# Group normalization on one core: VectorE's and TensorE's unrolled code put into loops with addresses from registers

## The chip, the cores and the metric

The kernel runs on one core of one Trainium2 chip. The metric is the device time of one execution in microseconds (us). Five engines of the core work from their own instruction streams and meet through semaphores: TensorE (PE; its weight loads are listed as PEld), VectorE (DVE), ScalarE (ACT), GpSimd (POOL) and SyncE (SP), which here only issues transfers. Sixteen DMA engines move data between the chip's memory (HBM) and the on-chip memory (SBUF); PSUM is the memory into which TensorE writes.

## The reference

Input x has the shape 128 x 1024 x 32 x 16 in bf16 (134 MB); the output has the same. The 1024 channels form 32 groups of 32. For each image and group, mean and variance are taken over 32 x 32 x 16 = 16384 values; then every channel is scaled and shifted.

```python
xr = x.reshape(B, G, C // G, H, W)
mu = xr.mean(axis=(2, 3, 4), keepdims=True)
var = ((xr - mu) ** 2).mean(axis=(2, 3, 4), keepdims=True)
xn = (xr - mu) / jnp.sqrt(var + 1e-5)
xn = xn.reshape(B, C, H, W)
return xn * g[None, :, None, None] + b[None, :, None, None]
```

## The kernel before

A tile is four images: 128 partitions (image and group), and in each the 16384 values of one group, that is 32 channels of 512 values (KC = 32, HW = 512). One tile has 4 MB. There are NT = 32 tiles and NBUF = 6 buffers `xt0` to `xt5`, in which a tile is loaded, scaled in place and stored. Tile i lies in buffer (i + ENTRY) mod 6 with ENTRY = 4.

The work on one tile, in order:

- SP issues the load (L163), which raises the buffer's semaphore `ld`.
- TensorE adds up the tile: 32 matmuls of 512 columns with the identity matrix `eye` as weights accumulate into the PSUM tile `pa` of this buffer (L194). The last one raises `s_pe`.
- VectorE sums the 512 columns of `pa` and multiplies by -1/16384, which gives `negmean` (the function `mean`, L211), and raises `s_mean`.
- ScalarE takes the square of x - mean over the tile in two halves with accumulation (L316), and makes the standard deviation of it (L330, L337); it raises `s_std`.
- VectorE takes the reciprocal (L223), makes 32 factors `scl` (L226) and 32 offsets `bia` (L233), and scales the tile channel by channel with 32 tensor_scalar instructions of 128 x 512 (L243). The last one raises `s_dve`.
- SP issues the store (L171), which raises the buffer's semaphore `st`.

VectorE's order within a step is: the mean of the next tile first, then reciprocal, factors, offsets and scalings of this tile. So ScalarE has the next mean before VectorE starts on its scalings.

SP's queue is one list, written out by the function `sync_program`. It begins with six loads. Later it goes in groups: three stores, each of which waits for `s_dve`, then three loads, each of which waits until the store of the tile that had its buffer is complete; then a tiny transfer (`spare`, L157) with a wait for the one before. The last six tiles are stored one after the other with no loads between.

TensorE, VectorE and ScalarE each run a loop of six trips, made by the function `loop`. A trip is two blocks of unrolled code, `first` (buffers 0 to 3) and `second` (buffers 4 and 5); the first trip enters at `second`. At the end of a trip the semaphores are counted down (L134), a register is raised (L135) and a branch goes back (L136). On TensorE and VectorE (`ahead=True`) the set-up (`prepare`) stands behind the loop and is reached by branches. All addresses in the unrolled code are constants: every buffer has its own instructions, and VectorE has `rstd`, `scl` and `bia` once per buffer.

Of the kernel before, what the change touches and what calls it, by code (L numbers as in the profile page):

```python
# [8 lines left out]
ALU = mybir.AluOpType  # L9
ENG = mybir.EngineType  # L10
F32 = mybir.dt.float32
BF16 = mybir.dt.bfloat16
# [3 lines left out]
EPS = 1e-5  # L16

NBUF = 6
RUN = 3
MM_FREE = 512  # L20
ENTRY = 4
SPARE = 32

# [2 lines left out]
def kernel(  # L26
# [7 lines left out]
    nc = tc.nc  # L34
    P = nc.NUM_PARTITIONS
    B0, C, H, W = x.shape
    G = NUM_GROUPS
    HW = H * W
    assert P % G == 0 and C % G == 0
    NS = P // G  # L40
    assert B0 % NS == 0
    NT = B0 // NS
    KC = C // G
    F = KC * HW
    inv_n = 1.0 / float(F)
    NMM = F // MM_FREE
    TRIPS = (NT + ENTRY) // NBUF
    assert F % MM_FREE == 0 and NT + ENTRY == TRIPS * NBUF

    x_v = x.rearrange("(t n) (g k) h w -> t (n g) (k h w)", n=NS, g=G)  # L50
    o_v = out.rearrange("(t n) (g k) h w -> t (n g) (k h w)", n=NS, g=G)
# [3 lines left out]
    sb = ctx.enter_context(tc.tile_pool(name="sb", bufs=1))  # L55
    ps = ctx.enter_context(tc.tile_pool(name="ps", bufs=1, space=bass.MemoryType.PSUM))

    xt = [sb.tile([P, F], BF16, name=f"xt{j}") for j in range(NBUF)]
    ja = sb.tile([P, F // 2], FP8, name="ja")
    jd = [sb.tile([P, MM_FREE], BF16, name=f"jd{n}") for n in range(2)]  # L60
    gb_b = sb.tile([G, 2, KC], BF16, name="gb_b")
# [8 lines left out]
    sq = sb.tile([P, 2 * NBUF], F32, name="sq")  # L70
    half = sb.tile([P, NBUF], F32, name="half")
    std = sb.tile([P, NBUF], F32, name="std")
    rstd = sb.tile([P, NBUF], F32, name="rstd")
    scl = [sb.tile([P, KC], F32, name=f"scl{j}") for j in range(NBUF)]
    bia = [sb.tile([P, KC], F32, name=f"bia{j}") for j in range(NBUF)]
    pa = [ps.tile([P, MM_FREE], F32, name=f"pa{j}") for j in range(NBUF)]
    gb_p = ps.tile([P, 2, KC], F32, name="gb_p")

    def sem(name):
        return tc.alloc_semaphore(name)  # L80
# [4 lines left out]
    s_pe, s_mean, s_sq, s_std = sem("s_pe"), sem("s_mean"), sem("s_sq"), sem("s_std")  # L85
    s_spare = sem("s_spare")
    s_dd, s_dve = sem("s_dd"), sem("s_dve")

    def buf(i):
        return (i + ENTRY) % NBUF  # L90

    def col(t, j):
        return t[:, j % NBUF : j % NBUF + 1]

    def loop(engine, prepare, step, settle, counts, ahead=False):

        es = bass.OrderedEngineSet([engine.engine])
        name = f"trip_{engine.engine.name}"
        first, middle, over, second, leave, past, begin, end = (
            f"{name}_{part}"
            for part in "first middle over second leave past begin end".split()
        )
        trip = nc.alloc_registers(f"{name}_n", engines=es)

        def set_up():
            prepare()  # L110
            for s, _, n in counts:
                if n:
                    engine.sem_inc(s, n)
            nc.regs_mov(trip, 0)
            nc.br(second, engines=es)

        if ahead:
            nc.regs_mov(trip, -1)
            nc.br_lt(trip, -1, on_true=first, on_false=middle, engines=es)
        else:  # L120
            set_up()
        with nc.body(first, valid_engines=es):
            for j in range(ENTRY):
                step(j)
            nc.br(middle if ahead else second, engines=es)
        if ahead:
            with nc.body(middle, valid_engines=es):
                nc.br_lt(trip, 0, on_true=over, on_false=second, engines=es)
        with nc.body(second, valid_engines=es):
            for j in range(ENTRY, NBUF):  # L130
                step(j)
            settle()
            for s, n, _ in counts:
                engine.sem_inc(s, -n)  # L134
            nc.regs_alu(trip, trip, 1, op=ALU.add)  # L135
            nc.br_lt(trip, TRIPS, on_true=first, on_false=leave, engines=es)  # L136
        with nc.body(leave, valid_engines=es):
            nc.br(past if ahead else end, engines=es)
        if ahead:
            with nc.body(over, valid_engines=es):  # L140
                nc.br(past, engines=es)
            with nc.body(past, valid_engines=es):
                nc.br_lt(trip, TRIPS, on_true=begin, on_false=end, engines=es)
            with nc.body(begin, valid_engines=es):
                set_up()
        nc.switch_bb(end)

    spacers = [0]
# [28 lines left out]
    def tensor_program(pe):  # L177
        def prepare():
            pe.wait_ge(s_gb, 32)
            pe.wait_ge(s_rep, 1)  # L180
            pe.matmul(  # L181
                out=gb_p[:].rearrange("p a k -> p (a k)"),
                lhsT=rep[:],
                rhs=gb_b[:].rearrange("q a k -> q (a k)"),
                start=True,
                stop=True,
            ).then_inc(s_pe, 1)
            pe.wait_ge(s_eye, 1)

        def step(j):  # L190
            pe.wait_ge(ld[j], 16)
            pe.sem_inc(ld[j], -16)  # L192
            for k in range(NMM):
                m = pe.matmul(  # L194
                    out=pa[j][:],
                    lhsT=eye[:],
                    rhs=xt[j][:, k * MM_FREE : (k + 1) * MM_FREE],
                    start=(k == 0),
                    stop=(k == NMM - 1),
                )  # L200
            m.then_inc(s_pe, 1)

        loop(pe, prepare, step, lambda: None, [], ahead=True)
        pe.drain()
        pe.sem_inc(s_pe, 1)

    def vector_program(dve):
        gam, bet = gb[:, 0, :], gb[:, 1, :]

        def mean(j):  # L210
            dve.tensor_scalar(  # L211
                out=jd[j % 2][:],
                in0=pa[j % NBUF][:],
                scalar1=-inv_n,
                scalar2=None,
                op0=ALU.mult,
                op1=ALU.add,
                accum_out=col(negmean, j),
            )._wait_ge(s_pe, j + 2).then_inc(s_mean, 1)

        def step(j):
            mean(j + 1)
            dve.reciprocal(out=col(rstd, j), in_=col(std, j))._wait_ge(  # L223
                s_std, j + 1
            ).then_inc(s_dd, 1)
            dve.tensor_scalar(  # L226
                out=scl[j][:],
                in0=gam,
                scalar1=col(rstd, j),
                scalar2=None,  # L230
                op0=ALU.mult,
            )._wait_ge(s_dd, 3 * j + 2).then_inc(s_dd, 1)
            dve.scalar_tensor_tensor(  # L233
                out=bia[j][:],
                in0=scl[j][:],
                scalar=col(negmean, j),
                in1=bet,
                op0=ALU.mult,
                op1=ALU.add,
            )._wait_ge(s_dd, 3 * j + 3).then_inc(s_dd, 1)  # L240
            for k in range(KC):
                span = xt[j][:, k * HW : (k + 1) * HW]
                m = dve.tensor_scalar(  # L243
                    out=span,
                    in0=span,
                    scalar1=scl[j][:, k : k + 1],
                    scalar2=bia[j][:, k : k + 1],
                    op0=ALU.mult,
                    op1=ALU.add,
                )  # L250
                if k == 0:
                    m._wait_ge(s_dd, 3 * j + 4)
                if k == KC - 2 and j == NBUF - 1:
                    m.then_inc(s_dd, 1)
            m.then_inc(s_dve, 1)

        def settle():
            dve.wait_ge(s_dd, 3 * NBUF + 2)

        def prepare():  # L260
            dve.memset(ones_b[:], 1.0).then_inc(s_set, 1)  # L261
            dve.tensor_copy(out=gb[:], in_=gb_p[:])._wait_ge(s_pe, 1).then_inc(s_dd, 1)  # L262
            dve.sem_inc(s_pe, ENTRY)
            mean(ENTRY)

        loop(
            dve,
            prepare,
            step,
            settle,  # L270
            [
                (s_pe, NBUF, 0),
                (s_std, NBUF, ENTRY),
                (s_dd, 3 * NBUF + 1, 3 * ENTRY),
            ],
            ahead=True,
        )

    def pool_program(pool):
        pool.affine_select(  # L280
            out=eye[:],
            in_=ones_b[:],
            pattern=[[-1, P]],
            compare_op=ALU.is_equal,
            fill=0.0,
            base=0,
            channel_multiplier=1,
        )._wait_ge(s_set, 1).then_inc(s_eye, 1)
        pool.affine_select(  # L289
            out=rep[:].rearrange("q (n a) -> q n a", n=NS),  # L290
            in_=ones_b[0:G, :].rearrange("q (n a) -> q n a", n=NS),
            pattern=[[0, NS], [-1, G]],
            compare_op=ALU.is_equal,
            fill=0.0,
            base=0,
            channel_multiplier=1,
        ).then_inc(s_rep, 1)
        pool.tensor_scalar(  # L298
            out=eps_t[:],
            in0=ones_b[:, 0:1],  # L300
            scalar1=EPS,
            scalar2=None,
            op0=ALU.mult,
        ).then_inc(s_set, 1)

    def scalar_program(act):
        act.dma_start(out=gb_b[:, 0, :], in_=g_v).then_inc(s_gb, 16)
# [86 lines left out]
```

## Time and profile before

| what | value |
|---|---|
| time of the runs, median of 3 | 633.19 us (632.77 to 633.47) |
| profiled execution, its time | 633.13 us |
| its span, first to last instruction | 631.3 us |
| busy: TensorE / VectorE / ScalarE | 255.1 / 375.8 / 476.2 us |
| moved by DMA | 268.57 MB, mean 425 GB/s |
| mean granted clock of TensorE | 0.729 of full speed |

In the lines of the profile that the prediction shows, L243 is line 243 of the program before. A line of a group of instructions gives the line, the engine, the operation, output and input with partitions x elements, how many there were (x1024), then busy time in all and nanoseconds of one, and at the end the idle time of the engine just before them and what ended it. A line of a timeline or a chain begins with the start and the duration in us. In the row of DMA shares each digit is a fortieth of the span in tenths. A `q` behind an engine's name stands for its sequencer, which handles branches, register operations and the issue of transfers.

### The profile page before, as it was taken

The numbers are of one execution on the slowest core, as the hardware profiler recorded it, in microseconds if no ns is written. First come the engines' busy times: TensorE is split into PE (matmuls) and PEld (weight loads), VectorE is DVE, ScalarE is ACT, GpSimd is POOL, SyncE is SP. The second block draws the span as 40 slices with busy tenths as digits, with TensorE's granted clock in tenths as the row PEclk, the third lists the DMA queues.
The fourth block names the chain that finished last, engine by engine and source line by source line (L and its number), as shares of the span: only waits on it lengthen the run. The fifth ranks groups of instructions, "written<-read, shape, count | busy, mean of one in ns | idle before, by whom it ended". The sixth has DMA issues, their size and how long they took to land. (4 is left out here: it accounts for less than half of the span.)

```text
span 631.3 us, 3704 instructions
## 1 busy us (share of the span) xinstructions
PE 255.1 (40%) x1009; PEld 105.4 (17%) x1025; DVE 375.8 (60%) x1188; ACT 476.2 (75%) x194; POOL 0.9 (0%) x7
## 2 busy tenths in 40 slices
PE   0967409009602750582087018404720770095000
PEld 0423103003201320230032003101300230032000
DVE  0057777774772777077727735770777177447771
ACT  0499999995994699189929965993899199649930
POOL 0000000000000000000000000000000000000000
PEclk9998858658855985687578659855975796598555
DMA  8999999999999999999999999999999999999996
GB/s 363 432 432 414 434 432 432 438 432 432 430 432 434 430 430 434 432 430 432 432 432 432 432 432 430 432 432 432 430 432 434 432 430 432 432 432 436 438 394 283
DMA packets 10756, 268.57 MB, mean 425 GB/s; under 512 B 2560, under 2 KB 2560, under 8 KB 2560
## 3 DMA queue, kind: packets, MB, share of 16 engines
q1 hardware_dynamic: 10656, 268.52, 99.0%
q10 hardware_dynamic: 96, 0.00, 0.0%
q14 instruction: 3, 0.02, 0.0%
q8 instruction: 1, 0.02, 0.0%
HBM read 134.30 MB, written 134.22 MB: 425 GB/s over the span
## 5 line engine op out<-in xcount | busy, mean ns | idle before, releaser
L316 ACT ACTIVATE ja<-xt,negmean 128x8192 fp8e5<-128x8192 bf16 x64 | 455.5, 7117 | 126.9 <-DVE jd L211 125.5
L194 PE MATMUL pa<-xt,eye 128*128 128x512 bf16 x1008 | 254.9, 414 | 312.4 <-PEq L192 310.9
L243 DVE TENSOR_SCALAR xt<-xt,scl,bia 128x512 bf16<-128x512 bf16 x1024 | 333.7, 408 | 1.2
L194 PEld LDWEIGHTS pa<-xt,eye 128*128 128x128 bf16 x1024 | 105.3, 105 | 461.6 <-issue 366.0
L211 DVE TENSOR_SCALAR_CACHE_REDUCE jd<-pa 128x512 bf16<-128x512 f32 x33 | 22.7, 687 | 147.3 <-PE pa L194 145.4
L223 DVE RECIPROCAL rstd<-std 128x1 f32<-128x1 f32 x32 | 5.2, 163 | 78.1 <-ACT std L337 78.1
L316 ACT ACTIVATION_READ_ACCUMULATOR ja<-xt,negmean 128x1 f32 x64 | 11.9, 186 | 0.0
L337 ACT ACTIVATE std<-sq,half 128x1 f32<-128x1 f32 x32 | 9.4, 295 | 1.0
L330 ACT ACTIVATE half<-sq,eps_t 128x1 f32<-128x1 f32 x32 | 8.9, 278 | 0.0
L233 DVE SCALAR_TENSOR_TENSOR bia<-scl,negmean,gb 128x32 f32<-128x32 f32 x32 | 8.1, 252 | 1.1
L226 DVE TENSOR_SCALAR scl<-gb,rstd 128x32 f32<-128x32 f32 x32 | 7.7, 241 | 1.1
L262 DVE COPY gb<-gb_p 128x64 f32<-128x64 f32 x1 | 0.2, 226 | 10.7 <-PE gb_p L181 10.7
L181 PE MATMUL gb_p<-gb_b,rep 32*128 32x64 bf16 x1 | 0.2, 231 | 12.5 <-DMA gb_b<-in_b_dram 12.5
L211 DVE DVE_READ_ACCUMULATOR jd<-pa 128x1 f32 x33 | 2.7, 83 | 0.0
L312 ACT ACT_TABLE_LOAD x1 | 1.3, 1283 | 1.9 <-issue 1.9
L181 PEld LDWEIGHTS gb_p<-gb_b,rep 32*128 32x128 bf16 x1 | 0.1, 100 | 12.5 <-DMA gb_b<-in_b_dram 12.5
L261 DVE MEMSET ones_b<- 128x128 bf16 x1 | 0.2, 165 | 1.9 <-issue 1.9
L289 POOL TENSOR_SCALAR_AFFINE_SELECT rep<-ones_b 32x128 bf16<-32x128 bf16 x1 | 0.3, 303 | 0.0
L280 POOL TENSOR_SCALAR_AFFINE_SELECT eye<-ones_b 128x128 bf16<-128x128 bf16 x1 | 0.3, 294 | 1.7 <-DVE ones_b L261 1.7
L312 ACT ACTIVATE warm<-eps_t 128x1 f32<-128x1 f32 x1 | 0.2, 203 | 0.0
L298 POOL TENSOR_SCALAR eps_t<-ones_b 128x1 f32<-128x1 bf16 x1 | 0.2, 205 | 0.0
L378 POOL MEMSET const-uint8-127<- 128x1 uint8 x1 | 0.1, 103 | 0.0
(3 smaller groups left out, 0.3 us busy)
## 6 DMA issues: line engine op xcount, KB each, us to landing
xt<-in_x_dram SPq DMA_DIRECT2D x32, 4096.0 KB, 29.1
out_dram<-xt SPq DMA_DIRECT2D x32, 4096.0 KB, 33.2
spare<-in_x_dram SPq DMA_DIRECT2D x10, 8.0 KB, 29.2
gb_b<-in_g_dram ACTq DMA_DIRECT2D x1, 2.0 KB, 7.8
gb_b<-in_b_dram ACTq DMA_DIRECT2D x1, 2.0 KB, 11.0
```

Of the source, the lines that this page charges most:

```text
L181: pe.matmul(out=gb_p[:].rearrange("p a k -> p (a k)"), lhsT=rep[:], rhs=gb_b[:].rearrange("q a k -> q (a k)"), start=True, stop=True,).the ...
L194: m = pe.matmul(out=pa[j][:], lhsT=eye[:], rhs=xt[j][:, k * MM_FREE : (k + 1) * MM_FREE], start=(k == 0), stop=(k == NMM - 1),)
L211: dve.tensor_scalar(out=jd[j % 2][:], in0=pa[j % NBUF][:], scalar1=-inv_n, scalar2=None, op0=ALU.mult, op1=ALU.add, accum_out=col(negmean, j),
L223: dve.reciprocal(out=col(rstd, j), in_=col(std, j))._wait_ge(s_std, j + 1).then_inc(s_dd, 1)
L226: dve.tensor_scalar(out=scl[j][:], in0=gam, scalar1=col(rstd, j), scalar2=None, op0=ALU.mult,)._wait_ge(s_dd, 3 * j + 2).then_inc(s_dd, 1)
L233: dve.scalar_tensor_tensor(out=bia[j][:], in0=scl[j][:], scalar=col(negmean, j), in1=bet, op0=ALU.mult, op1=ALU.add,)._wait_ge(s_dd, 3 * j ...
L243: m = dve.tensor_scalar(out=span, in0=span, scalar1=scl[j][:, k : k + 1], scalar2=bia[j][:, k : k + 1], op0=ALU.mult, op1=ALU.add,)
L280: pool.affine_select(out=eye[:], in_=ones_b[:], pattern=[[-1, P]], compare_op=ALU.is_equal, fill=0.0, base=0, channel_multiplier=1,)._wait ...
L312: act.activation(out=warm[:], in_=eps_t[:], func=ACT.Sqrt)
L316: m = act.activation(out=ja[:], in_=xt[j][:, h * F // 2 : (h + 1) * F // 2], func=ACT.Square, bias=col(negmean, j), scale=1.0, accum_out=s ...
L330: act.activation(out=col(half, j), in_=sq[:, 2 * j : 2 * j + 1], func=ACT.Identity, bias=eps_t[:], scale=inv_n,)._wait_ge(s_sq, 3 * j + 1) ...
L337: act.activation(out=col(std, j), in_=sq[:, 2 * j + 1 : 2 * j + 2], func=ACT.Sqrt, bias=col(half, j), scale=inv_n,)._wait_ge(s_sq, 3 * j + ...
```

## The change

TensorE and VectorE get short loops whose addresses come from registers.

- The six buffers become parts of one tile `x_all`, and the six PSUM tiles parts of `pa_all`, so that a register can choose among them. `rstd`, `scl` and `bia` exist once.
- VectorE loses the loop of trips. It has one loop over the tiles (`i` from 4 to 35, buffer `j = i % NBUF` in a register) with one step in it, and in the step a loop of four rounds with eight channels each (`SCALE_STEP`). A drain follows the rounds, and it raises `s_dve`. The semaphores are counted down by one or by three inside the step.
- TensorE keeps the loop of trips with its blocks. In each tile the first and the last matmul stand alone with constant addresses; the 30 between are ten rounds of three (`MM_STEP`) with an address from a register.
- `ahead` and the blocks that it needed are gone from `loop`; the set-up stands ahead of the loop. The gamma and beta matmul raises a semaphore of its own, `s_gbp`.
- POOL, ScalarE and SP have the same instructions in the same order.

In the program that is built, addresses are worked out by packed register instructions, each of which holds several additions and multiplications. In a round of VectorE each of the eight tensor_scalar instructions has two of them ahead (six and two operations; seven and three for the first of a round), and takes four addresses from registers; then follow one register addition and a compare-and-branch. In a round of TensorE there are three packed ones (six, five and five operations), a separate register addition for the first matmul, and a register addition and a compare-and-branch at the end. In VectorE's step there are further a packed one of six with a modulo and one of two ahead of the mean, a packed one of three ahead of the reciprocal, a register addition ahead of the offsets, and a register move and branch ahead of the rounds.

The core of the diff:

```diff
-    xt = [sb.tile([P, F], BF16, name=f"xt{j}") for j in range(NBUF)]
+    x_all = sb.tile([P, NBUF * F], BF16, name="x_all")
+    xt = [x_all[:, j * F : (j + 1) * F] for j in range(NBUF)]
...
+    rstd = sb.tile([P, 1], F32, name="rstd")
+    scl = sb.tile([P, KC], F32, name="scl")
+    bia = sb.tile([P, KC], F32, name="bia")
...
     def step(j):
         pe.wait_ge(ld[j], 16)
         pe.sem_inc(ld[j], -16)
-            for k in range(NMM):
-                m = pe.matmul(
...
+            add(xt[j][:, 0:MM_FREE], start=True)
+            with nc.Fori(0, (NMM - 2) // MM_STEP, 1, engines=...) as r:
+                for n in range(MM_STEP):
+                    add(xt[j][:, bass.ds((r * MM_STEP + n + 1) * MM_FREE, MM_FREE)])
+            add(xt[j][:, F - MM_FREE : F], stop=True).then_inc(s_pe, 1)
...
+        mean(ENTRY, 1)
+        with nc.Fori(ENTRY, NT + ENTRY, 1, engines=es) as i:
+            j = i % NBUF
+            mean((i + 1) % NBUF)
+            dve.reciprocal(out=rstd[:], in_=at(std, j, 1))._wait_ge(s_std, 1).then_inc(
+                s_dd, 1
+            )
+            dve.sem_inc(s_std, -1)
...
+            dve.wait_ge(s_dd, 3)
+            dve.sem_inc(s_dd, -3)
+            with nc.Fori(0, KC // SCALE_STEP, 1, engines=es) as r:
+                for n in range(SCALE_STEP):
+                    k = r * SCALE_STEP + n
+                    span = at(x_all, j * KC + k, HW)
+                    dve.tensor_scalar(
+                        out=span,
+                        in0=span,
+                        scalar1=at(scl, k, 1),
+                        scalar2=at(bia, k, 1),
+                        op0=ALU.mult,
+                        op1=ALU.add,
+                    )
+            dve.drain()
+            dve.sem_inc(s_dve, 1)
```

## The prediction

> **What bounds the kernel now.** I read the profile's page first, then the timeline of the DMA queue, the chain that ended last and a table by stage of the last 20 us. From the page:
>
> ```profile
> span 631.3 us, 3704 instructions
> PE 255.1 (40%) x1009; PEld 105.4 (17%) x1025; DVE 375.8 (60%) x1188; ACT 476.2 (75%) x194; POOL 0.9 (0%) x7
> ...
> DMA  8999999999999999999999999999999999999996
> ...
> L243 DVE TENSOR_SCALAR xt<-xt,scl,bia 128x512 bf16<-128x512 bf16 x1024 | 333.7, 408 | 1.2
> ...
> L223 DVE RECIPROCAL rstd<-std 128x1 f32<-128x1 f32 x32 | 5.2, 163 | 78.1 <-ACT std L337 78.1
> ```
>
> The DMA engines are full from the second slice to the last but one; no compute engine is over 75%. The timeline of SP's queue has the rhythm:
>
> ```profile
> 405.61 19.68 SPq L163 DMA_DIRECT2D xt<-in_x_dram  x3
> 425.34 0.43 SPq L157 DMA_DIRECT2D spare<-in_x_dram  x1
> 425.81 30.42 SPq L171 DMA_DIRECT2D out_dram<-xt  x3
> 464.00 19.68 SPq L163 DMA_DIRECT2D xt<-in_x_dram  x3
> ```
>
> Six transfers of one tile pass in 464.00 - 405.61 = 58.4 us, 9.73 us each, so a tile (in and out) costs the DMA 19.47 us. Transfers run in order: the first of the loads issued from 405.61 lands at about 434.7 (TensorE starts it then), the third at 454, two stores follow, and the third store, issued at 456.2, has its place only at about 474. Compute is some 17.5 us ahead of the DMA in mid-kernel, and VectorE is free to take up to 19.47 us a tile there. It takes 11.8 (mean 0.70, reciprocal to first scaling 0.76, scalings 10.43), and waits 3.07 for ScalarE, whose pace is 14.87 us a tile.
>
> At the ends there is no such cover. The chain that ended last:
>
> ```profile
> 553.47 7.12 PE pa L194 x28
> ...
> 560.61 0.71 DVE jd L211 x2
> ...
> 606.85 10.43 DVE xt L243 x32
> ```
>
> and the table by stage (columns: window; us; busy time of PE, PEld, DVE, ACT, POOL; clock; DMA share; GB/s):
>
> ```profile
> 614.00:616.00 2.00, 0.00 (x0) 0.00 (x0) 2.00 (x8) 0.00 (x0) 0.00 (x0) 0.50 0.27 115
> 616.00:618.00 2.00, 0.00 (x0) 0.00 (x0) 1.28 (x4) 0.00 (x0) 0.00 (x0) 0.50 0.27 115
> 618.00:620.00 2.00, 0.00 (x0) 0.00 (x0) 0.00 (x0) 0.00 (x0) 0.00 (x0) 0.50 1.12 475
> ```
>
> The DMA runs dry from 614 to 618: the last store waits for the last scaling (617.3). So what is added between the landing of tile 29 (551.8) and 617.3 is added to the span.
>
> The price of a sequencer's register instruction comes from the loop edges:
>
> ```profile
> L135 PEldq ALU_OP  x6: 36/36/42, 27.8 to 575.9; - x6
> ...
> L135 DVEq ALU_OP  x6: 40/40/58, 66.1 to 617.3; - x6
> ```
>
> Start to start in the trace's records, an ALU_OP of VectorE takes 78 ns (162.871 to 162.949), of PE 102 (106.608 to 106.710); a semaphore increment of VectorE 95. A taken branch on VectorE: 305 ns from its start (162.949) to the next operation's (163.254); a branch not taken, 81 (617.359 to 617.440). PE's taken branch executes 208 ns, about 250 to the next start.
>
> **The change, part by part.** It moves no DMA and no ScalarE instruction; SP, POOL and ScalarE keep their order.
>
> *VectorE's scaling.* The 32 tensor_scalar instructions stay, at 323 ns start to start (41.408 to 41.731), but each now has in front of it two packed register instructions (six and two operations, giving four addresses). No trace here shows such a packed one. Bounds: the six cost between one ALU_OP (78) and six (468); I take 78 + 5 x 13 = 143, a third of the 40 ns execution for each further operation, as fetch is paid once. The two: 78 to 156, taken 91. Issuing the tensor_scalar itself: 78 (an ALU_OP) to 323 (the sequencer keeps up now); with four addresses from registers I take 160. Sum 0.39 us, taken 0.40; bounds 0.234 (the engine's 0.323 then decides) and 0.947. I stay nearer the low end, because the nearest row is one whole instruction, and 38 of its 78 ns are not execution and here paid once for several operations. Each of four rounds ends with an ALU_OP, a taken branch (305, less the issue already counted) and two more packed operations: about 0.33, so 1.3 a tile (0 if queued work covers it, 1.5 at most). The loop: 32 x 0.40 + 1.3 = 14.1, +3.7 on 10.43.
>
> [...]
>
> *Around it, once a tile.* Before the first scaling: two semaphore decrements (0.095 each), a wait for the third s_dd, a register move, a branch, a packed pair, an issue; partly beside the small operations: 0.8 (0.3 to 1.5). They queue ahead of the scalings, for which the store waits. At the tile's end: drain, ALU_OP, taken branch, two packed instructions with the modulo, issue of the mean: 0.8 (0.4 to 1.5), before 0. So VectorE needs D = 0.70 + 1.55 + 14.1 + 0.8 = 17.15 us a tile: over ScalarE's 14.87, under the DMA's 19.47.
>
> *TensorE.* A round of three matmuls has three packed instructions, two ALU_OPs, a taken branch. With 145 for a packed one (36 execution + 66 fetch + 4 x 11) and 100 for the matmul with its weight load: 3 x 245 + 204 + 250 = 1.19 us; ten rounds and the rest 12.4 us a tile. Now the first tile of a burst takes 9.24 (15.00 to 24.24), starting at half clock (428 ns a matmul, later 216). So +3.0; low 0 (the sequencer keeps ahead), high 2.73 us a round with all 16 packed operations at 102, 27 us a tile. In mid-kernel +3.0 lies under the 17.5; only tiles 0 and 29 count.
>
> *The rest at nothing:* one rstd, scl and bia instead of six, since VectorE runs in order; the set-up without its detour (branches of 0.1 us, under the first load's 15 us).
>
> *Sum.* Start: store 0 was ready at 51.2, now 51.2 + 3.0 + 0.8 + 3.7 = 58.7, before its place at 62.3 (six loads). Store 1 follows one D later, 75.85; issue and first bytes take 1.8; the DMA is free at 72.0: 5.6 idle. Store 4 at 75.85 + 3 x 17.15 + 1.8 = 129.1, its place (120.6 + 5.6) is 126.2: 2.9 idle. Together 8.5. After that VectorE, faster than the DMA, falls behind no further. End: the mean of tile 29 is 3.0 later; from there to the last scaling it took 617.28 - 560.61 = 56.7, now four VectorE steps less the last turn, 4 x 17.15 - 0.8 = 67.8: +11.1. Span 631.3 + 8.5 + 3.0 + 11.1 = 653.9. The profiled execution took 633.13, 1.8 over its span (median of the runs 633.19), so **656 us**. With s from 0.34 to 0.47 us a scaling this case runs from 640 to 680.
>
> **Rivals.**
> *VectorE's sequencer keeps ahead* (s at most 0.33). For: the 0.234 bound, and queued scalings that would hide the round ends. Against: three instructions would have to average 108 ns, hardly above the 78 of the cheapest. Then D is about 14, ScalarE keeps the pace, and only 3.0 + 0.8 + 0.5 at the end remain: 637 us. [...]
>
> *VectorE becomes the bound* (s over 0.47, D over 19.47). For: eight operations at 78 alone are 0.62. Every tile then waits for VectorE: step 0 begins at about 43, and 43 + 32 D - 1.5 + 14 + 1.8. s = 0.50 gives D = 20.4 and 710 us, 0.60 gives 812, 0.70 gives 915.
>
> *TensorE becomes the bound*: a round over 1.9 us makes a tile longer than 19.47; at 27 us some 900. Against: packing would save nothing.
>
> *Not slower*: both sequencers stay ahead, PE's too. Its place is tile 29's matmuls: at up to 0.9 us a round against 0.65 to 1.28 that the array needs, the first tile, half of it at the slow clock, ends no later; and VectorE as in the first rival. What is left is 1 us of loop edges: 634, within 0.2%. Against: branch and two ALU_OPs alone are 0.45 of a round. Nothing on the final chain gets shorter, so a gain has hardly a place.
>
> **How the numbers follow.** The forecast's case 0.50; hidden sequencer 0.17; VectorE the bound 0.22; TensorE the bound 0.04; not slower 0.05; faster by something unseen 0.02. About 0.2% (1.3 us) is what a measurement of this kernel can tell from no change. Slower 0.93, same 0.05, faster 0.02. The range from 635 to 800 leaves out the last two and the upper part of the two bound cases, about 0.2.
>
> **What would show it.** Scalings start to start: 400 ns on average inside a round (right), 323 (first rival), over 470 (second). The wait of RECIPROCAL for ScalarE, 78.1 us now, almost gone, and ScalarE's squares waiting for the mean instead. The first tile of a burst on PE near 12 us. DMA gaps near 72 and 127 us and a longer one before the last stores, with full slices between; gaps in every group of three would mean VectorE has passed the DMA. Wrong, if the span moves by under 3 us or by over 50.

## The result, and the profile after

The changed kernel takes 640.02 us (median of 5 runs, 639.88 to 640.09) against 633.19, a ratio of 1.0108 with a 95% interval of 1.0094 to 1.0122. It is slower, as forecast, but by 6.8 us and not by 22.8. The profiled execution took 640.06 us with a span of 638.3, so the span to explain is 638.3 - 631.3 = 7.0 us.

From the page of the changed kernel:

```profile
span 638.3 us, 8230 instructions
PE 284.6 (45%) x1025; PEld 103.3 (16%) x1025; DVE 394.8 (62%) x1188; ACT 476.4 (75%) x194; POOL 0.9 (0%) x7
...
DMA  8999999999999999999999999999999999999866
...
L247 DVE TENSOR_SCALAR x_all<-x_all,scl,bia x1024 | 351.1, 413 | 40.0 <-issue 22.1
...
L222 DVE RECIPROCAL rstd<-std 128x1 f32 x32 | 5.2, 162 | 21.0 <-ACT std L319 21.0
```

The DMA row shows no hole before the last three slices: the gaps that the prediction expected near 72 and 127 us are not there. VectorE's wait for ScalarE has shrunk from 78.1 to 21.0 us, but it is still there, so ScalarE, with 14.87 us a tile, still sets the pace and VectorE stays just under it. The instructions recorded have gone from 3704 to 8230 with the engines' own instructions unchanged; that number will matter.

What became of the scalings is in the instructions of line 247 and of the loop's line 243 (operation, count, least/median/largest ns, first and last start; below, the engine's idle time by what ended it, with the number of times):

```profile
L247 DVEq FUSED_REGOPS  x1920: 46/64/179, 40.2 to 624.4; - x192
L247 DVE TENSOR_SCALAR x_all<-x_all,scl,bia x1024: 411/413/416, 40.3 to 624.5; - x171
...
  issue: 22.1, 96
  DVEq L242: 17.9, 32
```
```profile
L243 DVEq FUSED_REGOPS  x128: 204/204/204, 39.9 to 621.9; - x128
...
L243 DVEq COMPARE_BRANCH  x128: 50/56/69, 42.8 to 624.6; - x128
```

The packed instruction of six operations takes 179 ns, that of two 46 to 53; at the first scaling of a round, that of seven takes 204 and that of three 64. Start to start inside a round the trace has 210 ns for the packed six (615.316 to 615.526), 100 for the packed two up to the tensor_scalar (615.626), and 22 from there to the next: 332 ns a scaling, where it was 323. The 96 idle times are the three round ends inside each of 32 tiles; the 32 are the first scalings of a tile, 0.56 us each. The chain of work that ended last shows a round end:

```profile
615.63 0.07 DVE x_all L247
615.73 0.06 DVEq L243
615.78 0.14 issue
615.92 0.20 DVEq L243
616.15 0.06 DVEq L247
616.22 0.05 issue
616.27 0.20 DVE x_all L247
```

The step from 615.63 to 616.27 is 0.64 us, 0.315 more than one inside a round. The branch has 0.19 of it (615.73 to 615.92).

On the chain at the end, with tile 29's landing as the time at which the last part of its load is in:

| piece | before | after | difference |
|---|---|---|---|
| landing of tile 29 | 551.68 | 556.72 | +5.04 |
| landing to the start of its mean (TensorE) | 8.9 | 9.8 | +0.86 |
| that mean to the last scaling's end (617.28, 624.94) | 56.67 | 58.43 | +1.76 |
| last scaling's end to the span's end | 14.0 | 13.4 | -0.65 |

The 1.76 are 0.52 between reciprocal and first scaling (1.29 against 0.76) and 1.23 in the 32 scalings (11.66 against 10.43). So the new code costs 2.6 us on this chain, and the larger part, 5 us, is a load that lands later, although the compute engines and the DMA row show nothing that would hold it up.

It is held up on one of the sixteen DMA engines. A transfer raises its semaphore once for each of them, and the trace has the time of each:

| load of tile 29 | first | median | 15th | last |
|---|---|---|---|---|
| before | 546.59 | 546.90 | 551.13 | 551.68 |
| after | 546.73 | 547.17 | 548.77 | 556.72 |

Fifteen of them are there within 0.3 us of before, or sooner. In the kernel before, four engines lag behind the median, by 2.9, 4.2, 4.2 and 4.8 us; after, two lag by 1.5 and 1.6 and one by 9.6. I call *lag* the last landing less the median. After grows it by about 1.0 us per group of three tiles (1.0 at 101 us, 4.2 at 247, 6.6 at 392, 9.6 at 547), before by about 0.3 from 2.3 at 101 us. One engine of sixteen busy alone can be seen in the table by stage, too (share of the DMA in the last but one column; 1/16 is 0.06):

```profile
618.00:620.00 2.00, 0.00 (x0) 0.00 (x0) 1.77 (x7) 0.00 (x0) 0.00 (x0) 0.50 1.22 524
620.00:622.00 2.00, 0.00 (x0) 0.00 (x0) 1.98 (x6) 0.00 (x0) 0.00 (x0) 0.50 0.08 33
622.00:624.00 2.00, 0.00 (x0) 0.00 (x0) 1.79 (x6) 0.00 (x0) 0.00 (x0) 0.50 0.04 16
```

SP's timeline shows it as a longer rhythm. A load waits for a store to be complete on all sixteen engines, and three loads now take 20.1 us to be issued instead of 19.68:

```profile
408.97 20.12 SPq L144 DMA_DIRECT2D x_all<-in_x_dram  x3
429.14 0.43 SPq L138 DMA_DIRECT2D spare<-in_x_dram  x1
429.61 32.85 SPq L152 DMA_DIRECT2D out_dram<-x_all  x3
468.13 20.11 SPq L144 DMA_DIRECT2D x_all<-in_x_dram  x3
```

A group takes 468.13 - 408.97 = 59.16 us, where it took 58.39.

### The profile page after: what moved, and what is told of

The parts are those of the page before. It is cut to its first block, busy times and chain, and to the rows that moved or that the text cites. A ratio compares the mean times of both kernels' runs of the same rounds, so it can differ in the third digit from the quotient of the medians.

```text
span 638.3 us, 8230 instructions
## 1 busy us (share of the span) xinstructions
PE 284.6 (45%) x1025; PEld 103.3 (16%) x1025; DVE 394.8 (62%) x1188; ACT 476.4 (75%) x194; POOL 0.9 (0%) x7
## 5 line engine op out<-in xcount | busy, mean ns | idle before, releaser
L298 ACT ACTIVATE ja<-x_all,negmean 128x8192 fp8e5<-128x8192 bf16 x64 | 455.6, 7119 | 132.6 <-DVE jd L203 131.3
L176 PE MATMUL pa_all<-x_all,eye 128*128 (+1 forms) x1024 | 284.4, 403 | 290.2 <-PEq L173 267.3
L247 DVE TENSOR_SCALAR x_all<-x_all,scl,bia x1024 | 351.1, 413 | 40.0 <-issue 22.1
L176 PEld LDWEIGHTS pa_all<-x_all,eye 128*128 128x128 bf16 x1024 | 103.2, 101 | 471.3 <-issue 421.6
L203 DVE TENSOR_SCALAR_CACHE_REDUCE jd<-pa_all 128x512 bf16 (+1 forms) x33 | 22.8, 692 | 155.8 <-PE pa_all L176 141.9
L222 DVE RECIPROCAL rstd<-std 128x1 f32 x32 | 5.2, 162 | 21.0 <-ACT std L319 21.0
L298 ACT ACTIVATION_READ_ACCUMULATOR ja<-x_all,negmean 128x1 f32 x64 | 12.0, 188 | 0.0
L203 DVE DVE_READ_ACCUMULATOR jd<-pa_all (+1 forms) x33 | 2.8, 83 | 0.0
```

The source lines that it names most:

```text
L176: return pe.matmul(out=pa[j][:], lhsT=eye[:], rhs=rhs, start=start, stop=stop)
L203: dve.tensor_scalar(out=jd[n][:], in0=at(pa_all, j, MM_FREE), scalar1=-inv_n, scalar2=None, op0=ALU.mult, op1=ALU.add, accum_out=at(negmea ...
L222: dve.reciprocal(out=rstd[:], in_=at(std, j, 1))._wait_ge(s_std, 1).then_inc(s_dd, 1)
L247: dve.tensor_scalar(out=span, in0=span, scalar1=at(scl, k, 1), scalar2=at(bia, k, 1), op0=ALU.mult, op1=ALU.add,)
L298: m = act.activation(out=ja[:], in_=xt[j][:, h * F // 2 : (h + 1) * F // 2], func=ACT.Square, bias=col(negmean, j), scale=1.0, accum_out=s ...
```

## The experiments

My theory (A in the expectations) was that the lag grows with the number of instructions that run, whatever they do; the rivals put the later landing on TensorE's stretched bursts (B), or on each program's start (C). The runs that bear on it, times in us (each ratio is to the kernel before on the same chip):

| kernel | time | ratio to before [95%] | instructions | lag, tile 29 | last scaling ends | store of tile 30 complete | last store complete |
|---|---|---|---|---|---|---|---|
| before | 633.19 | | 3704 | 4.78 | 617.28 | 619.57 | 629.81 |
| after | 640.02 | 1.0108 [1.0094, 1.0122] | 8230 | 9.55 | 624.94 | 625.94 | 636.79 |
| e1 | 637.55 | 1.0068 [1.0051, 1.0085] | 6328 | 7.49 | 621.44 | 623.48 | 633.72 |
| e2 | 635.20 | 1.0029 [1.0019, 1.0040] | 5622 | 5.66 | 619.12 | 621.28 | 631.53 |
| e3 | 635.69 | 1.0033 [1.0020, 1.0046] | 6721 | 6.75 | 619.19 | 622.21 | 632.46 |
| e5 | 637.04 | 1.0055 [1.0038, 1.0072] | 6918 | 7.60 | 621.37 | 623.63 | 633.87 |
| e6 | 633.07 | 1.0000 [0.9990, 1.0009] | 3707 | 4.48 | 617.44 | 619.84 | 629.62 |
| e7 | 636.28 | 1.0051 [1.0035, 1.0068] | 6885 | 7.19 | 620.91 | 622.78 | 633.03 |
| e8 | 640.32 | 1.0118 [1.0101, 1.0135] | 10605 | 11.43 | 623.68 | 626.69 | 636.92 |
| e9 | 660.49 | 1.0435 [1.0418, 1.0453] | 8998 | 7.23 | 645.22 | 638.44 | 657.09 |
| e12 | 633.32 | 1.0004 [0.9995, 1.0013] | 1800 | 5.39 | 610.06 | 620.35 | 630.03 |
| e14 | 638.00 | 1.0077 [1.0060, 1.0093] | 7920 | 9.18 | 621.62 | 624.46 | 634.71 |
| e15 | 637.86 | 1.0074 [1.0057, 1.0091] | 7921 | 8.98 | 622.54 | 624.34 | 634.59 |

### One half of the change alone

**VectorE's loops alone (e1).** The changed kernel with TensorE's tile unrolled as before:

```diff
-            add(xt[j][:, 0:MM_FREE], start=True)
-            with nc.Fori(0, (NMM - 2) // MM_STEP, 1, ...) as r:
...
+            for k in range(NMM):
+                m = pe.matmul(... rhs=xt[j][:, k * MM_FREE : (k + 1) * MM_FREE], ...)
```

> VectorE as after, TensorE unrolled as before (32 matmuls a tile with constant addresses). Theory A: one of the sixteen DMA engines falls behind in proportion to the number of instructions that the sequencers go through while stores run (before 3704 in the trace, after 8230; its lag behind the median engine at the landing of tile 29 is 4.8 us before, 9.5 after). VectorE has some 2500 of the 4526 added instructions, so lag +2.6, landing of tile 29 near 554.4, and with the 1.75 us of VectorE at the end (0.52 ahead of the scalings, 1.23 in them) about 637.2. Theory B: the lag comes from TensorE's stretched bursts beside the stores; then it goes away here: landing of tile 29 near 551.7, 635.0 in all. Theory C: the lag is a matter of each program's start and has no tie to the instructions: no claim, anything from 635 to 640.

**TensorE's loops alone (e2).** The kernel before, with the new `step` of TensorE in it (the same diff the other way round) and the six buffers as parts of one tile `x_all`.

> TensorE with rounds of three as after, VectorE unrolled as before. Theory A: some 1900 added instructions, lag +2.0; 0.86 us for the longer first tile of a burst; about 636.0. Theory B: the whole lag of after, +5, and 0.86: 639. Both: scalings at 323 ns, last reciprocal to last scaling 11.2 us as before.

Measured: 637.55 and 635.20. Each half brings a part, +4.1 and +1.8 against the kernel before on the same chip (633.43), and both lags lie between those of before and after. The TensorE half has its 0.86 us (mean of tile 29 9.8 us after the landing) and nothing like the 3.0 of the forecast. Tile 29 lands at 554.40 and 552.67: neither half has the later landing to itself, which speaks for A. But the TensorE half has less of it than A gave it: its landing is 1.0 us later and not 2.0.

**32 channels unrolled (e5).** The changed kernel without the rounds; only the buffer is in a register, so a scaling has one packed instruction:

```diff
-            with nc.Fori(0, KC // SCALE_STEP, 1, engines=es) as r:
-                for n in range(SCALE_STEP):
-                    k = r * SCALE_STEP + n
...
+            for k in range(KC):
...
-                        scalar1=at(scl, k, 1),
+                    scalar1=scl[:, k : k + 1],
```

> After, but VectorE's 32 scalings of a tile stand in a row with constant channel offsets: one packed register instruction ahead of each instead of two, no ends of rounds, scl and bia at constant addresses. Scalings should come at the engine's own 323 ns again (10.4 us from first to last end, instead of 11.66), so 1.2 us less at the end. Theory A: about 1440 instructions fewer than after, lag 1.5 smaller: 637.4. Theories B and C: the lag as after, 638.8.

Measured: 637.04. The scalings stand 0.323 us apart as in the kernel before, and the 32 of the last tile take 10.42 us instead of 11.66: the sequencer keeps ahead with one packed instruction and not with two. The time is 3.0 below the changed kernel's: with 1312 instructions fewer the lag is 1.9 smaller, and the last scalings are 1.2 shorter.

### Is it the number of instructions?

**GpSimd spins (e3, e7, e8).** The kernel before, and GpSimd, which is otherwise idle after 3 us, runs a loop of drains (500 or 1150 turns) or of packed register instructions (530 turns). It touches no data:

```diff
+        with nc.Fori(0, 500, 1, engines=bass.OrderedEngineSet([pool.engine])):
+            for _ in range(4):
+                pool.drain()
```

> The kernel before, and beside it GpSimd, idle otherwise, goes 500 times round a loop of four drains, a register addition and a branch: some 3000 instructions that touch no data and that nobody waits for. Theory A: landing of tile 29 some 3 us later than before (551.7), the rest unchanged: 636. Theories B and C: 633.2 as before.

> The kernel before, with GpSimd in a loop of five packed register instructions (28 operations) and a branch, for nearly the whole span: about 3200 instructions, 6 a microsecond, GpSimd's sequencer busy all the time. Theory A1 (the number of instructions counts, one record of each for the trace): the last load lands some 2.2 us later, 635.6. Theory A2 (the time that a sequencer is busy counts): as e8, +4.7, 638.1.

> As e3 (GpSimd in a loop of four drains, an addition and a branch), but 1150 turns instead of 500: some 6900 instructions until about 540 us instead of 3000 until 237. Theory A: the last engine's lag goes on growing by 1.0 us in each group of three tiles instead of 0.4 after 237 us; tile 29 lands some 4.7 us later than before, 638.1.

Measured: 635.69, 636.28 and 640.32. The e8 loop, which ends at 541 us, makes the kernel before as slow as the changed one, with TensorE, VectorE and the transfers untouched. In e3 the lag grows by 1.0 a group while GpSimd spins (until 237 us) and by about 0.4 afterwards. e7 holds some 28 operations a turn in six instructions and its sequencer is busy for 351 us instead of 235; its time lies nearer to what the number of instructions gave (635.6) than to what busy time gave (638.1). But the 638.1 took the loop to run nearly to the end, and it ended at 353 us, so the time alone doesn't decide between the two; the packets below do. Nothing in these runs moves data, changes the kernel's own addresses or adds to the code of another engine, so those causes fall.

**Fewer instructions (e12).** The kernel before, of each tile only the first and last matmul:

```diff
-            for k in range(NMM):
+            for k in (0, NMM - 1):
```

> The kernel before with only the first and the last of the 32 matmuls of each tile (30 of 32 parts of the sum behind the mean are left out): 1920 fewer instructions in the record, TensorE's code much shorter, every transfer as before. A tile's matmuls take under 1 us instead of 7 to 9, so the last scaling ends some 8 us earlier and the last store lies ready when the one before it ends. Theory A (the end is set by the slowest of the 16 DMA engines, whose lag grows with the instructions that run): the lag shrinks by 0.9 to 1.5 us per thousand instructions, 1.7 to 2.9 us in all, and up to 2 us more if the lag of the first 50 us, which came with fetched code, goes too: 628.5 to 631.5. Theory B (the slowest DMA engine sets the end, but its lag has nothing to do with the instructions): 633.1, as with the last store in four parts. Theory C (the chain of compute sets the end): some 8 us less, 625.

Measured: 633.32, no difference, with half of the instructions:

```profile
span 631.5 us, 1800 instructions
...
PE 32.6 (5%) x65; PEld 4.5 (1%) x65; DVE 375.7 (59%) x1188; ACT 476.2 (75%) x194; POOL 0.9 (0%) x7
```

Theory A's number failed: the lag is 5.4, not 2 to 3. Theory C failed too: the last scaling ends 7.2 us earlier and nothing comes of it. So the 4.8 us of lag in the kernel before have another cause, which none of these runs removed; what e12 did to the engine that instructions hold up is told below.

**Memsets instead of drains (e13, e14, e15).** e12 left open whether only instructions count that a sequencer handles itself. e13 put 160 turns of 16 tiny memsets into GpSimd from 2 us on:

```diff
+        with nc.Fori(0, 160, 1, engines=bass.OrderedEngineSet([pool.engine])):
+            for n in range(16):
+                pool.memset(spin[:, n : n + 1], 1.0)
+            pool.drain()
```

> The kernel before, with GpSimd running a loop beside it from 2 us on, as in the run with 500 turns, but of engine instructions: 160 turns of 16 tiny memsets (128x1 each, in a tile that nothing else uses), a drain and the loop's edge, 2560 memsets and 480 other instructions. Nothing else of the kernel changes. Theory A (any recorded instruction delays the slowest DMA engine): as many instructions as in the run with drains, so the same: 635.5 to 636. Theory B (only instructions that the sequencer handles by itself do it, as the run with two matmuls a tile suggests): a sixth of it, 633.5. [...]

Measured: 636.46, ratio 1.0055 [1.0041, 1.0069], and inconclusive. The memsets slowed VectorE (a scaling took 432 ns on average, not 408) at the start, where it was busy for 81.7 us of the 100 from 100 to 200 us (59.2 of the next 100); every DMA engine then loads tile 29 some 2.5 us later (median 549.44). Its lag is 4.94, where e3 with about as many instructions has 6.75. A lagging engine catches up in gaps of the others, as over the changed kernel's last three stores (lag 9.8, 4.8, 0.8), and I take the 4.94 to be that. So the same was done in mid-kernel, where VectorE has slack (11.8 us of work a tile in the kernel before, 19.47 for the DMA), with 4200 instructions of either kind and a wait in front:

```diff
+        pool.wait_ge(st[4], 32)
```

> The kernel before, and GpSimd, once the second store from buffer 4 is complete (at about 190 us), runs 221 turns of 16 tiny memsets, a drain and the loop's edge: 3536 memsets, 663 others. VectorE has over 7 us of slack a tile there, so its slowing should move no transfer. Theory A (any instruction delays one DMA engine's stores): lag of tile 29's load 7 to 8 us instead of 4.8, time 635.5 to 637. Theory B (only instructions that the sequencer handles itself): 663 of them add under 0.5 us, 633.2 to 633.5, lag under 5.3.

> The same with 700 turns of four drains and the loop's edge, 4200 instructions that the sequencer handles itself, from about 190 to 520 us. Both theories: lag of tile 29's load 7 to 8 us, time 635.5 to 637. If instead the time stays at 633.2, what counted in the earlier runs was the stretch in which GpSimd ran and not the number of its instructions.

The groups of instructions show what ran, and when:

```profile
L309 POOL MEMSET spin<- x3536: 98/98/287, 181.6 to 372.7; 128x1 f32 x197
```
```profile
L308 POOLq DRAIN  x2800: 34/34/41, 181.6 to 509.2; - x187
```

Measured: 638.00 and 637.86, both with a median landing of tile 29 as before (546.83 and 546.89) and a lag of 9.2 and 9.0. The lag follows the loops: with memsets it goes from 4.49 at 285 us to 7.84 at 392 (1.8 a group) and slows down when they end; with drains from 4.45 at 324 to 8.51 at 489 (1.4 a group). Less the 0.3 of the kernel before, and by 22 and 12.8 instructions a microsecond, that is 1.2 and 1.5 ns for each instruction. So memsets count as drains do. The changed kernel's 4526 further instructions at this price are 5.4 to 6.8 us; its lag is 4.8 larger.

**Which engine it is, and in which transfers.** The trace also has each packet of the transfers. A tile is 128 packets of 32 KB, eight for each DMA engine, and a packet starts as the one before it on its engine ends, so the sixteen engines can be told apart. From 295 to 321 us, in every kernel of the table below, all packets of fifteen engines take 1.213 us. Those of one engine take longer, and by how much depends on the instructions that run only while they belong to stores:

| kernel | instructions per us, 295 to 303.5 us | store packets of this engine, longer by | its load packets (311.5 to 321 us), longer by | this engine behind the median at tile 29 |
|---|---|---|---|---|
| e12 | 2.9 | 5 ns | 3 ns | 2.8 us |
| before | 2.6 | 7 ns | 4 ns | 4.0 us |
| e1 | 8.1 | 24 ns | 4 ns | 7.3 us |
| after | 8.0 | 25 ns | 3 ns | 9.5 us |
| e8 | 15.4 | 45 ns | 4 ns | 11.3 us |
| e15 | 15.4 | 48 ns | 5 ns | 8.9 us |
| e14 | 24.9 | 79 ns | 4 ns | 9.1 us |

The last column goes by the end of the engine's last packet of the tile. In stores, at one packet in 1.21 us, this is 1.5 to 2.6 ns for each instruction. In loads the instructions cost next to nothing: beside the load packets e12 runs 1.5 of them a microsecond and e14 24.

TensorE's instructions count as well. From 280.5 to 288 us TensorE works on a tile beside a store, and the packets of this engine are longer by 0.17 us in all in the kernel before (78 instructions, 55 of them TensorE's), by 0.23 in e2 (118 and 96) and by nothing in e12 (24 and none). And it is the number that counts, not the busy time: in e7 the sequencer is in its loop all the time as in e8, with three quarters of the instructions, and in three stretches between 179 and 321 us the packets are longer by 1.27 us against 1.62.

This settles e12. With 1904 instructions fewer this engine lags by 2.8 us and not by 4.0, the way theory A has it, if by less than its 1.7. But in the kernel before it isn't the slowest: at tile 29 another, whose packets all take 1.213 us from 527 to 550 us too, is 4.8 us behind, and 5.4 in e12. From before to after the engine's own lag grows by 5.5 us (4.0 to 9.5), 1.2 ns for each of the 4526 instructions, which is the price found with GpSimd.

### What sets the end

**The last store in four parts (e6).** The kernel before, where the last store is issued in quarters, each as soon as its eight channels are scaled:

```diff
+            if i == NT - 1:
+                for n in range(parts):
+                    sync.wait_ge(s_dve, earlier + n + 1)
+                    cols = slice(n * F // parts, (n + 1) * F // parts)
+                    sync.dma_start(out=o_v[i][:, cols], in_=xt[j][:, cols]).then_inc(
+                        st[j], 16
+                    )
...
```

> The kernel before, with the store of the last tile in four parts of eight channels, each issued as soon as its scalings are done (VectorE raises s_dve three times more in buffer 5). If the span ends with the last scaling and then a whole store, as the prediction read it, the last 4 MB (12.5 us from issue to landing) become 1 MB after the last scaling: about 7 us less, 626. If the DMA has other work at the end, or four transfers cost as much as one, less than 2 us.

Measured: 633.07, ratio 1.0000 [0.9990, 1.0009]. The hole of the DMA from 614 to 618 us is filled, as the table by stage shows, and a new one stands behind it:

```profile
616.00:618.00 2.00, 0.00 (x0) 0.00 (x0) 1.44 (x5) 0.00 (x0) 0.00 (x0) 0.50 1.04 438
...
622.00:624.00 2.00, 0.00 (x0) 0.00 (x0) 0.00 (x0) 0.00 (x0) 0.00 (x0) 0.50 1.01 426
624.00:626.00 2.00, 0.00 (x0) 0.00 (x0) 0.00 (x0) 0.00 (x0) 0.00 (x0) 0.50 0.22 90
626.00:628.00 2.00, 0.00 (x0) 0.00 (x0) 0.00 (x0) 0.00 (x0) 0.00 (x0) 0.50 0.19 82
628.00:630.00 2.00, 0.00 (x0) 0.00 (x0) 0.00 (x0) 0.00 (x0) 0.00 (x0) 0.50 0.07 29
```

The median engine has finished the last store at 624.76 instead of 628.32, but the slowest at 629.62 instead of 629.81: for the last 5 us some three engines of sixteen work, then one. In the kernel before, four engines worked on through this hole (share 0.27), the slowest among them, so the slowest engine never ran dry, and its work is the bound of the span. The last two columns of the table say the same of the other kernels: the last store is complete 9.7 to 10.3 us behind the store before it on the slowest engine, in all of them but the changed one (10.85) and e9 (18.65), where the last scaling comes late. So in the changed kernel the two limits all but coincide: the slowest engine comes free at 625.94, and the last scaling is done at 624.94 and its store's data start about 1.3 us later (the median engine's landing at 636.00, less 9.73 for a transfer). That e1, with the round ends, and e5, without them, are within 0.5 us of each other follows from this too: in both the slowest engine sets the end.

### Is the price of a scaling the sequencer's?

**Half the width (e11).** The changed kernel with scalings of 256 columns; the other half of each channel is left unscaled:

```diff
-                    span = at(x_all, j * KC + k, HW)
+                    span = x_all[:, bass.ds((j * KC + k) * HW, HW // 2)]
```

> The changed kernel, but each scaling takes only 256 of the channel's 512 columns (the other half of the output is left unscaled). It measures the cost of one scaling on VectorE's sequencer by itself. Theory A (in the changed kernel the sequencer sets the distance of 0.332 us, just above the 0.323 that the engine needs): the distance stays 0.32 to 0.34 although the engine needs about half; the scalings of a tile take 11.4 us as before (11.66 less half a scaling's own time), the time stays 640 within 1.0. Theory B (the engine sets the distance, and the sequencer has more in hand than 0.01 us a scaling): the distance falls towards 0.2, a tile's scalings to about 7.5, the end of the chain by about 4 us: 636. The prediction's price (0.40 us, of which 0.16 for issuing the scaling itself) would give a distance of 0.40.

Measured: 640.00 (one run, 633.25 for the kernel before). The scalings' own time falls by 67 ns and their distance stays at 332:

```profile
L247 DVE TENSOR_SCALAR x_all<-x_all,scl,bia x1024: 345/346/349, 40.5 to 624.2; - x171
...
  issue: 28.5, 96
```

Theory A holds: VectorE's sequencer sets the distance, 332 ns, with 9 ns over what the engine needs for 512 columns.

**Shorter rounds (e9, e10).** `SCALE_STEP` is 2 or 1 instead of 8, so that a tile has 16 or 32 round ends.

> After, with 16 rounds of two channels in VectorE's inner loop instead of four of eight. A round's end costs 0.315 us in the trace of after, so the scalings take 15.4 us a tile instead of 11.66 and VectorE 18.2, over ScalarE's 14.87 and under the DMA's 19.47: the case that the prediction took for the likeliest. By its sum (idle DMA at stores 1 and 4, four VectorE steps at the end) 659 without the lag and 664 with it. If VectorE's step is hidden in mid-kernel and at the end too, 643.

> The changed kernel with rounds of one scaling, so 32 round ends a tile. From the distance of 0.332 us inside a round, 0.315 more at a round's end, and 3.1 for what is outside the rounds: VectorE needs 32 x 0.647 = 20.7 and 20.7 + 3.1 - 0.6 = 23.2 us a tile, more than the DMA's 19.5, so VectorE is the bound. By the prediction's formula for that case, 43 + 32 x 23.2 - 1.5 + 14 + 1.8 = 800 us (785 if a round end costs 0.30, as rounds of two suggest), with VectorE waiting for nobody and gaps on the DMA at every tile. A lag of one DMA engine adds nothing then, since the transfers no longer touch. Rival: a round of one has nothing queued ahead, so its packed instructions and the issue lie bare, 0.40 + 0.33 = 0.73 a round: D = 25.9, 886 us.

Measured: 660.49 and 765.64 (one run). Their DMA rows:

```profile
DMA  9999899799999999999999999999999999997655
```
```profile
DMA  9996697399969969996996999699699969963555
```

With rounds of two VectorE needs 17.93 us a tile (reciprocal to reciprocal, 38.83, 56.80, 74.73): the forecast's case with nearly its D. Then its terms are there: holes in slices 5 and 8, after which every engine is 10.0 us later (median landing of tile 29 556.89 against 546.90; 8.5 forecast with D = 17.15), full slices between, and from the landing of tile 29 on its slowest engine (564.12) to the last scaling 81.1 us against 65.6, +15.5 (3.0 + 11.1 forecast). The lag adds 2.4 (7.2 against 4.8). With rounds of one VectorE is the bound, 22.27 us a tile with a hole in every group, as the second rival had it; a round takes 0.623, so the round end is a little cheaper (0.29), and my 785 to 800 was too high because D was not 23.2 and the first step began at 39, not 43.

## Why the prediction was right or wrong

**Right: the direction, and where it would show.** Mid-kernel compute stayed hidden, and the added time shows at the end. But the sign that the forecast named, VectorE's wait for ScalarE almost gone, didn't come: it fell to 21.0 us and stayed. And the reading that all that is added between tile 29's landing and the last scaling is added to the span was about 1 us off: in the kernel before, the last store could start at 618.6 (its median landing less 9.73), and the slowest DMA engine came free only at 619.57.

**The step that failed: the issue of a scaling, taken at 160 ns, measured at 22.** The forecast summed 143 + 91 + 160 to s = 0.40. The trace has 210 + 100 + 22 = 0.332. The packed six are dearer than I took them, but an instruction with four addresses from registers costs next to nothing on top of them. Everything behind it hung on s: with 0.332 VectorE stays under ScalarE's 14.87 us a tile, so the 8.5 us of idle DMA at the start did not come, and the end paid 1.76 and not 11.1 us. e9 shows that the rest of that sum was sound once a tile takes VectorE 17.9 us.

**The same error on TensorE.** A round of three was put at 1.19 us with 100 ns for each matmul's issue. Branch to branch it takes 0.897 to 0.937 (557.621 to 565.851), and the first tile costs 0.86 more, not 3.0. The rows of the loop:

```profile
L181 PEldq FUSED_REGOPS  x320: 78/78/83, 13.6 to 584.7; - x160
...
L181 PEldq COMPARE_BRANCH  x320: 76/208/232, 14.3 to 585.3; - x160
```

**Right, or nearly, in size:** the round end (0.33, measured 0.315), the way to the first scaling (0.8, measured 0.52) and the tile's end (0.8, measured 0.75). The round end came out right partly by luck: its branch is cheaper than the row I took, 190 ns to the next operation and not 305, and the packed seven behind it, at 204 ns, are dearer. No run shows the 1.8 us that the sum took for issue and first bytes: in the kernel before, the last store's data start about 1.3 us after the last scaling (617.28 to 618.6, the median landing less 9.73).

**Missing: the lag.** "It moves no DMA" was true of the transfers and not of their time. No term of the sum, and no rival, had instructions delaying the stores of one of sixteen DMA engines while they run; 5.0 of the 7.0 us came this way. The kernel before showed a lag in its trace (the sixteen landings of a load spread over 5 us), and I read only the mean share of the DMA. That 640 is also the lower end that the forecast gave its own case is luck, since most of it was paid for something that the sum didn't have.

**The nearest rival** was the hidden sequencer, 637 us. It was not hidden, only nearly so (332 against 323), and its sum of 4.3 us was not what was paid: 2.6 on the chain, less 0.65, and 5.0 for the lag. Scalings queued ahead, which it had to hide the round ends, covered nothing here: 22.1 us of idle engine in 96 round ends, as a sequencer that needs 332 ns for what the engine does in 323 didn't get ahead.

**Open.** Every execution timed here was also recorded, so the runs can't tell whether it is the running of an instruction or its record that holds up a DMA engine. Why only the store packets of one engine are held up is open too, and so is what makes the 4.8 us of lag of another engine in the kernel before; none of the runs brought a version faster than it.

## What to carry to other kernels

Before a loop with register addresses is priced, look whether the packed register instructions of one turn fit under the engine's own time for it: here two of them (332 ns) just didn't fit under 323, one did (323 ns a scaling in e5), and the round ends came on top, 0.315 us each; no run has round ends with a turn that fits. When transfers are the bound, read the landings of all DMA engines one by one: here the slowest one set when a buffer came free and, in all kernels of the table but the changed one and e9, when the last store was complete, and work that filled a hole on the others brought nothing (e6: ratio 1.0000, e12: 1.0004). And instructions are not free because their engine is idle: 6901 on GpSimd, idle otherwise, made the kernel before 1.2% slower (e8), and the 4526 of the change delayed a landing by about 5 us.

## What was not expected of the hardware

- One DMA engine of sixteen falls behind while instructions run on the core: 1.2 to 1.5 ns for each of GpSimd's over stores and loads together, memsets (22 a microsecond) and drains (12.8) alike, which came to 4.3 us for 4200 of them and 6.6 for 6900.
- Only its store packets are longer, by 1.5 to 2.6 ns for each instruction; its load packets are 3 to 5 ns longer whether 1.5 or 24 instructions a microsecond run beside them.
- In the kernel before, four engines already lag, by 2.9 to 4.8 us at 547 us; 1904 fewer recorded instructions, nearly all of TensorE, didn't help the slowest (5.4).
- GpSimd's memsets of one column, 98 ns each, lengthened VectorE's scalings (408 to 435 ns on average over the whole kernel in e14).
